# Attention and two dense blocks on one core: a list scheduler that treats VectorE and GpSimd as sharing one port exclusively, and float64 weights rebiased on ScalarE

## Chip, cores and metric

The kernel runs on one core of one Trainium2 chip. The metric is the device time of a launch in microseconds (us). Matmuls run on TensorE (PE in the rows), its weight loads beside them (PEld), elementwise work on VectorE (DVE), ScalarE (ACT) and GpSimd (POOL); transfers are issued from SyncE (SP).

## What is computed

Three stages, each fed by the one before; batch 4, widths as in the code:

```python
# 1: windowed attention with 32 global tokens (8 heads, 512 local tokens, head_dim 64)
s_g = scale * q_g @ concat(k_g, k_l).T;  out_g = softmax(s_g) @ concat(v_g, v_l)
s_ll = where(abs(i - j) <= 32, scale * q_l @ k_l.T, -1e9)
out_l = softmax(concat(scale * q_l @ k_g.T, s_ll)) @ concat(v_g, v_l)
x = concat(out_g, out_l) as (4, 576, 512)
# 2: first dense block, w_in (512, 1024), conv_w (3, 1024), w_out (1024, 512)
h = maximum(x @ w_in, 0)
gate = 1 / (1 + exp(-(3-tap convolution of h over the sequence)))
x = (h * gate) @ w_out
# 3: second dense block
xk = mu_k * x + (1 - mu_k) * x_prev;  xr = mu_r * x + (1 - mu_r) * x_prev
k = maximum(xk @ w_k, 0)
out = 1 / (1 + exp(-(xr @ w_r))) * ((k * k) @ w_v)
```

## The kernel before, in words

**Attention.** The 32 (batch, head) pairs are handled as 16 units of two heads, four units to a batch; unit u belongs to batch u // 4. For each unit `attend` issues scores (`s`, matmuls at L460 and L469), a masked minimum on VectorE (L484, eight passes of 128 columns), exponentials on ScalarE (L491), transposes of the exponentials (`pe`, L500), their copy to SBUF (`eT`, L503, ScalarE or VectorE), the product with v (`o`, L510), the division (L520 to L522, VectorE), a transpose (`X`, L541) and the split of x into a high and a low part (`xh`, L548, ScalarE or VectorE; `xl`, L551, VectorE). For each second unit `glob` does the same for the global tokens (`sg`, `eg`, `peg`, `egT`, `Xg`).

**First dense block,** `dense(b)` for each batch: eight H groups m (`ph`, matmuls at L856), relu (L880 on ScalarE, L882 on VectorE), a convolution of three taps (the first at L891, L893 or L895, on ScalarE, VectorE or GpSimd; the other two at L898 on VectorE), sigmoid (L904, ScalarE), a product `mu` (L907, VectorE or GpSimd) and the split of the gate into `gh` (L914, ScalarE or VectorE) and `gl` (L919, GpSimd or VectorE). Two m share one pair of gate tiles: `gh0_6` and `gl0_6` hold m = 6 and 7 of batch 0. Then the O matmuls (`po`, L957) need all gates; the results go to DRAM.

**Second dense block,** `moe2`: chunks of 384 tokens, the last of 256. Each has a K stage (`pk`, L1094, eight m, each followed by a relu at L1112 on ScalarE, a square at L1117 and a split into `k2h` and `k2l`, L1124 and L1129), an R stage (`pr`, L1160) and a V stage (`pv`, L1197) that needs `k2h` and `k2l`.

All dense matmuls are three products of high and low parts.

**Weights** come as float64, seen as pairs of 32-bit words. `narrow_tasks` (L701) makes fp32 of a piece of 128 x 512 (or 256) in passes: absolute value of the upper word (L712 on ScalarE, L714 on VectorE), max with a constant (L717, VectorE or GpSimd), a shift with a mask (L721, VectorE), and two passes that bring in the sign and the lower word's bits (L727, VectorE). A split into a high part (L792) and a low part (L795, GpSimd or VectorE) follows.

**Order.** All of this is recorded as tasks with an engine, a planned cost, alternatives on other engines, needs and buffers. `Plan.keys` gives due times, worked back from constants (`SLOT`, `LEAD`, `GAP`, `STEP0`, `LAG_TE`, `LAG_PV`, ...); `Plan.schedule` then takes, step by step, from the tasks that could start within `WINDOW` of the earliest start the one due first. For a task with alternatives it takes the engine with the earliest planned end plus a bias of the engine and phase (`DVE_BIAS`, `ACT_BIAS`, `POOL_BIAS`; five phases by `PHASES`). The tasks are emitted in that order under `manual_schedule`, so each engine runs its instructions in the planned order, and waits for what they need; planned times themselves enforce nothing. Before, a planned cost on VectorE or GpSimd grew by a factor (`PORT`, `POOL_SLOW`) for the time in which the other was planned busy (`shared`).

Of the kernel before, what the change touches and what calls it, by code (L numbers as in the profile page):

```python
# [54 lines left out]
H_FRAC = 0.5  # L55
LAG_TE = 5000
LAG_PV = 10538
LAG_G = 7061
# [1275 lines left out]
```

## Time and profile before

| | |
|---|---|
| median of 3 runs | 604.93 us (604.0 to 605.22) |
| profiled execution | 603.86 us |
| its span, first to last instruction | 602.1 us |
| mean granted TensorE clock | 0.949 |
| busy: PE, DVE, ACT, POOL | 565.3 us (94%), 395.7 (66%), 285.5 (47%), 228.2 (38%) |

Busy shares are of the span; PE's is no statement that TensorE works at full speed. A row of the chain of waits is a stretch in which the end of the program depended on that engine. Rows by line and form give busy time, mean duration and what ended the engine's idle time before them.

### The profile page before, as it was taken

What the parts mean: (1) busy time and instruction counts of PE and PEld (TensorE: products, weight loads), DVE (VectorE), ACT (ScalarE), POOL (GpSimd) and SP (SyncE); (2) the same over time, 40 slices, a digit from 0 to 9 for tenths busy, and PEclk for the clock granted to TensorE, in tenths of its full rate; (3) what the DMA queues carried; (4) which work ended last, traced back from release to release, by engine and by line L of the source; (5) the groups of instructions that cost most, each with busy time, mean ns of one, the idle gap of its engine ahead of it and who ended that gap; (6) DMA issues with size and microseconds to landing.
All of it is one profiled execution on the core that took longest, in us unless ns stands there. A gap on an engine that the chain in (4) does not pass through costs nothing. (4 is left out here: it accounts for less than half of the span.)

```text
span 602.1 us, 14503 instructions
## 1 busy us (share of the span) xinstructions
PE 565.3 (94%) x5790; PEld 515.3 (86%) x5790; DVE 395.7 (66%) x969; ACT 285.5 (47%) x632; POOL 228.2 (38%) x320
## 2 busy tenths in 40 slices
PE   8697957997999979999999899999999999999998
PEld 6585946996989879889899799889889899898897
DVE  3689999847699954999958976441826637434211
ACT  4585856614588623677466634504305225134040
POOL 3647767622243302333111554937602203203150
PEclk8787986797999979999999989999999999999999
DMA  8957701567515675005480432020110200100000
GB/s 310 339 195 246 275 10 52 179 180 233 179 54 197 193 255 174 20 3 167 170 255 16 137 126 64 8 81 18 39 67 1 62 35 1 53 19 1 36 19 35
DMA packets 34627, 67.80 MB, mean 113 GB/s; under 512 B 5120, under 2 KB 14592, under 8 KB 34560
## 3 DMA queue, kind: packets, MB, share of 16 engines
q1 hardware_dynamic: 34560, 66.88, 33.4%
q8 instruction: 45, 0.74, 0.5%
q14 instruction: 22, 0.18, 0.1%
HBM read 52.71 MB, written 14.16 MB: 111 GB/s over the span
## 5 line engine op out<-in xcount | busy, mean ns | idle before, releaser
L856 PE MATMUL ph<-x,win_hi 128*128 128x256 f32 (+1 forms) x512 | 102.4, 298 | 0.0
L957 PE MATMUL po<-gl,wout_hi 128*128 128x256 f32 (+1 forms) x256 | 77.8, 304 | 7.1 <-POOL gl L919 5.2
L957 PE MATMUL po<-gh,wout_hi 128*128 128x256 f32 (+1 forms) x256 | 79.9, 312 | 2.8 <-ACT gh L914 2.8
L856 PEld LDWEIGHTS ph<-x,win_hi 128*128 128x128 f32 x512 | 81.2, 192 | 1.4
L957 PE MATMUL po<-gh,wout_lo 128*128 128x256 f32 (+1 forms) x256 | 76.9, 300 | 0.0
L856 PE MATMUL ph<-x,win_lo 128*128 128x256 f32 (+1 forms) x256 | 74.2, 290 | 0.0
L1112 ACT ACTIVATE robuf<-pk 128x384 f32<-128x384 f32 (+1 forms) x48 | 22.7, 472 | 91.8 <-PE pk L1094 91.4
L898 DVE SCALAR_TENSOR_TENSOR c<-h,convw,c 128x544 f32<-128x544 f32 x64 | 60.2, 959 | 4.6 <-POOL h L877 2.3
L1094 PE MATMUL pk<-xkh,wkk_lo 128*128 128x384 f32 (+1 forms) x192 | 62.7, 327 | 0.0
L1094 PE MATMUL pk<-xkh,wkk_hi 128*128 128x384 f32 (+1 forms) x192 | 62.7, 327 | 0.0
L1094 PE MATMUL pk<-xkl,wkk_hi 128*128 128x384 f32 (+1 forms) x192 | 62.7, 327 | 0.0
L957 PEld LDWEIGHTS po<-gl,wout_hi 128*128 128x128 f32 x256 | 51.7, 202 | 8.0 <-POOL gl L919 5.9
L957 PEld LDWEIGHTS po<-gh,wout_hi 128*128 128x128 f32 x256 | 51.7, 202 | 4.5 <-ACT gh L914 3.2
L1197 PE MATMUL pv<-wvv_lo,k2h 128*128 128x512 f32 (+1 forms) x144 | 54.4, 378 | 0.0
L1197 PE MATMUL pv<-wvv_hi,k2h 128*128 128x512 f32 (+1 forms) x144 | 54.4, 378 | 0.0
L1197 PE MATMUL pv<-wvv_hi,k2l 128*128 128x512 f32 (+1 forms) x144 | 54.4, 377 | 0.0
L1210 DVE TENSOR_TENSOR robuf<-pv,robuf 128x512 f32<-128x512 f32 (+1 forms) x18 | 11.9, 661 | 63.5 <-PE pv L1197 63.4
L957 PEld LDWEIGHTS po<-gh,wout_lo 128*128 128x128 f32 x256 | 51.7, 202 | 0.0
L856 PEld LDWEIGHTS ph<-x,win_lo 128*128 128x128 f32 x256 | 49.0, 192 | 0.0
L491 ACT ACTIVATE e<-e 128x128 f32<-128x128 f32 x128 | 39.8, 392 | 8.8 <-DVE e L484 8.7
L1160 PE MATMUL pr<-wrr_hi,xrbuf 128*128 128x512 f32 x136 | 43.7, 395 | 0.0
L1094 PEld LDWEIGHTS pk<-xkl,wkk_hi 128*128 128x128 f32 x192 | 36.1, 188 | 0.2
(224 smaller groups left out, 1294.9 us busy)
## 6 DMA issues: line engine op xcount, KB each, us to landing
v<-in_v_l_dram SPq DMA_DIRECT2D x16, 910.0 KB, 7.1
x2d<-xo SPq DMA_DIRECT2D x16, 272.5 KB, 2.9
qT<-in_q_l_dram SPq DMA_DIRECT2D x16, 256.0 KB, 3.6
kT<-in_k_l_dram SPq DMA_DIRECT2D x16, 256.0 KB, 4.7
wout_0r<-in_moe_w_out_dram SPq DMA_DIRECT2D x8, 512.0 KB, 4.5
out_dram<-robuf SPq DMA_DIRECT2D x16, 256.0 KB, 2.0
win_0r<-in_moe_w_in_dram SPq DMA_DIRECT2D x4, 512.0 KB, 8.0
win_512r<-in_moe_w_in_dram SPq DMA_DIRECT2D x4, 512.0 KB, 7.3
```

The source lines that it names most:

```text
L491: nc.scalar.activation(be.tile[:, P * i : P * (i + 1)], be.tile[:, P * i : P * (i + 1)], AF.Exp, bias=be.tile[:, SL + i : SL + i + 1], sca ...
L856: nc.tensor.matmul(pm, lhsT=w[:, k, P * m : P * (m + 1)], rhs=x[:, s0:s1], start=(k == 0 and n == 0), stop=(k == KT - 1 and n == 2),)
L898: e.scalar_tensor_tensor(bc.tile, bh.tile[:, k : k + S], convw[:, FT * k + m : FT * k + m + 1], bc.tile, op0=ALU.mult, op1=ALU.add,)
L957: nc.tensor.matmul(pm, lhsT=w[:, k, P * m : P * (m + 1)], rhs=g[:, k % 2, s0:s1], start=(k == 0 and n == 0), stop=(k == FT - 1 and n == 2),)
L1094: nc.tensor.matmul(bp.tile[:, :n], lhsT=w[:, k, P * m : P * (m + 1)], rhs=x[:, :n], start=(k == 0 and i == 0), stop=(k == KT - 1 and i == 2),)
L1112: e.activation(kk()[:, :n], bp.tile[:, :n], AF.Relu)
L1160: nc.tensor.matmul(bp.tile, lhsT=x[:, P * j : P * (j + 1)], rhs=w[:, k], start=(k == 0 and i == 0), stop=(k == KT - 1 and i == 2),)
L1197: nc.tensor.matmul(bp.tile, lhsT=x, rhs=w[:, k, c0:c1], start=(k == 0 and i == 0), stop=(k == FT - 1 and i == 2),)
L1210: nc.vector.tensor_mul(o()[:, c0:c1], bp.tile, r()[:, c0:c1])
```

## The change

The planner gets a resource `PORT`: a planned pass of VectorE whose kind is in the set `PORT` holds it for its whole planned duration, one of GpSimd for 0.9 of it (0.5 for first taps and for the normalisation `gn`, 0 for a memset of ones), and neither starts, in the plan, before it is free. The factors go. In `narrow_tasks` the absolute value and the max are replaced by one ScalarE pass that multiplies the upper word, read as fp32, by 2^-112; the shift loses its mask, and the sign is taken with a mask of one bit. Constants of the due times and biases change. Lines up to 700 of before stand 5 lines higher after, those from 717 on 17 lines: L957 becomes L940, L919 L902, L898 L881, L795 L778, L727 L713 and L721 L709.

```diff
-F64_MIN = float(np.array(0x38000000, np.uint32).view(np.float32))
+REBIAS = 2.0**-112
...
-SLOT = 72484
-LEAD = 14181
+SLOT = 67927
+LEAD = 18186
...
-POOL_BIAS = (6, 0, 235, 0, 113)
+POOL_BIAS = (514, 564, 295, 354, -3480)
...
-                    if o[0] == "DVE":
-                        c = shared(c, free.get("POOL", 0.0) - x, PORT.get(t.kind, 1.0))
-                    elif o[0] == "POOL":
-                        c = shared(c, free.get("DVE", 0.0) - x if dve_port else 0.0, POOL_SLOW)
+                    if holds_port(o[0], t.kind):
+                        x = max(x, free.get("PORT", 0.0))
...
-            if t.eng == "DVE":
-                dve_port = PORT.get(t.kind, 1.0) > 1.0
+            if h := holds_port(t.eng, t.kind):
+                free["PORT"] = max(free.get("PORT", 0.0), t.start + h * t.cost)
...
-def shared(cost, left, slow):
-
-    if left <= 0:
-        return cost
-    return cost * slow if left >= cost * slow else left + cost - left / slow
+def holds_port(eng, kind):
+
+    if eng == "POOL":
+        return 0.0 if kind == "on" else 0.5 if kind in ("cv", "gn") else 0.9
+    return 1.0 if eng == "DVE" and kind in PORT else 0.0
...
-        def fabs(e):
+        def fmag():
             state["mag"] = alloc(bmag, [P, max(n, EST)], F32, f"{nm}m")[:, :n]
-            hw = state["raw"][:, :n, 1]
-            if e is nc.scalar:
-                e.activation(state["mag"], hw.bitcast(F32), AF.Abs)
-            else:
-                e.tensor_scalar(state["mag"].bitcast(I32), hw, 0x7FFFFFFF, None, op0=ALU.bitwise_and)
-
-        def fmax(e):
-            e.tensor_scalar(state["mag"], state["mag"], F64_MIN, None, op0=ALU.max)
+            nc.scalar.activation(state["mag"], state["raw"][:, :n, 1].bitcast(F32), AF.Copy, scale=REBIAS)
...
-            nc.vector.tensor_scalar(
-                bits, bits, 3, 0x3FFFFFF8, op0=ALU.logical_shift_left, op1=ALU.bitwise_and
-            )
+            nc.vector.tensor_scalar(bits, bits, 3, None, op0=ALU.logical_shift_left)
...
-        c = add("ACT", 40 + 480 * f, lambda: fabs(nc.scalar), deps=[a], take=[bmag], use=[braw], name=f"abs{nm}",
-                alts=[("DVE", 60 + 275 * f, lambda: fabs(nc.vector))])
-        c = add("DVE", 60 + 275 * f, lambda: fmax(nc.vector), deps=[c], use=[bmag], name=f"max{nm}",
-                alts=[("POOL", 70 + 1386 * f, lambda: fmax(nc.gpsimd))])
+        c = add("ACT", 90 + 490 * f, fmag, deps=[a], take=[bmag], use=[braw], name=f"abs{nm}")
         c = add("DVE", 60 + 275 * f, fshift, deps=[c], use=[bmag], name=f"shl{nm}")
-        c = add("DVE", 68 + 534 * f, lambda: for_(1, -0x40000000, ALU.bitwise_and), deps=[c],
+        c = add("DVE", 68 + 534 * f, lambda: for_(1, -0x80000000, ALU.bitwise_and), deps=[c],
```

The order of the instructions changes on every engine. Three places follow; names carry the unit or batch (`s8_0`: scores of unit 8, first half; `po0_0_0`: O of batch 0) and a buffer number.

TensorE behind the first O matmuls of batch 0, before; the first matmul that needs `gl0_6` follows only behind the scores of units 6 and 7:

```order
L957 MATMUL po0_1_1_1504<-gl0_0_1407,wout_hi_165 128x288
L957 MATMUL po0_1_1_1504<-gh0_0_1357,wout_lo_166 128x288
L510 MATMUL o4_1_1514<-v4_842,eT4_1_1002 32x65 x16
L500 MATMUL pe5_0_1533<-ident_94,e5_0_1075 128x128 x4
L500 MATMUL pe5_1_1540<-ident_94,e5_1_1091 128x128 x4
L638 MATMUL peg5_0_1554<-ident_94,eg5_1131 128x128 x3
L510 MATMUL o5_0_1561<-v5_1057,eT5_0_1549 32x65 x16
L510 MATMUL o5_1_1583<-v5_1057,eT5_1_1552 32x65 x16
L541 MATMUL X4_1605<-ident_94,xn4_1545 128x128 x4
L638 MATMUL peg5_1_1618<-ident_94,eg5_1131 128x128 x3
```

The changed kernel's TensorE, up to and into the first O matmuls of batch 0:

```order
L464 MATMUL s8_0_1722<-kT8_1180,qT8_1016 32x96 x4
L464 MATMUL s8_1_1723<-kT8_1180,qT8_1016 32x96 x4
L495 MATMUL pe6_1_1774<-ident_94,e6_1_1591 128x128 x4
L505 MATMUL o6_0_1781<-v6_1097,eT6_0_1765 32x65 x16
L495 MATMUL pe7_0_1809<-ident_94,e7_0_1676 128x128 x4
L505 MATMUL o6_1_1818<-v6_1097,eT6_1_1800 32x65 x16
L940 MATMUL po0_0_0_1837<-gh0_0_1321,wout_hi_165 128x256
L940 MATMUL po0_0_0_1837<-gl0_0_1560,wout_hi_165 128x256
L940 MATMUL po0_0_0_1837<-gh0_0_1321,wout_lo_166 128x256
```

Scores of unit 8 and the second stage of units 6 and 7 stand ahead of O where before units 4 and 5 did. Between here and the first matmul that needs `gl0_6` stand also the scores of unit 9 and the rest of units 6 to 8.

GpSimd while `w_out` is narrowed, before (`wout3_0m` is a piece of w_out in work, `c0_0` the conv and gate tile of m = 0):

```order
L717 TENSOR_SCALAR wout3_0m_1195<-wout3_0m_1195 128x512
L876 MEMSET h0_2_1217 128x1
L877 MEMSET h0_2_1217 128x1
L907 TENSOR_TENSOR c0_0_1170<-c0_0_1170,h0_0_1137 128x544
L895 TENSOR_SCALAR c0_1_1265<-h0_1_1181,convw_96 128x544
L717 TENSOR_SCALAR wout4_0m_1256<-wout4_0m_1256 128x512
L876 MEMSET h0_4_1287 128x1
L877 MEMSET h0_4_1287 128x1
L795 TENSOR_TENSOR wout_lo_166<-wout2_0m_1142,wout_hi_165 128x512
```

The same place after:

```order
L890 TENSOR_TENSOR c0_2_1237<-c0_2_1237,h0_2_1212 128x544
L859 MEMSET h0_6_1361 128x1
L860 MEMSET h0_6_1361 128x1
L859 MEMSET h0_5_1372 128x1
L860 MEMSET h0_5_1372 128x1
L778 TENSOR_TENSOR wout_lo_166<-wout0_0m_1078,wout_hi_165 128x512
L778 TENSOR_TENSOR wout_lo_166<-wout2_0m_1223,wout_hi_165 128x512
```

The max passes and first taps are gone there; products, low parts and memsets stay.

VectorE at the last conv taps of batch 0 (`c0_5` to `c0_7`), before, with the division of unit 5 (`xn5`) and the masks of unit 6 behind them:

```order
L898 SCALAR_TENSOR_TENSOR c0_5_1625<-h0_5_1409,convw_96,c0_5_1625 128x544
L898 SCALAR_TENSOR_TENSOR c0_7_1674<-h0_7_1446,convw_96,c0_7_1674 128x544
L898 SCALAR_TENSOR_TENSOR c0_5_1625<-h0_5_1409,convw_96,c0_5_1625 128x544
L898 SCALAR_TENSOR_TENSOR c0_7_1674<-h0_7_1446,convw_96,c0_7_1674 128x544
L520 TENSOR_SCALAR xn5_1614<-o5_1_1583 128x4
L521 RECIPROCAL xn5_1614<-xn5_1614 128x4
L522 TENSOR_TENSOR xn5_1614<-o5_1_1583,xn5_1614 128x4x64
L484 ISA e6_0_1717<-s6_0_1632,mask_95 128x128
L484 ISA e6_0_1717 128x1
```

The same place after:

```order
L881 SCALAR_TENSOR_TENSOR c0_5_1947<-h0_5_1372,convw_96,c0_5_1947 128x544
L881 SCALAR_TENSOR_TENSOR c0_6_1835<-h0_6_1361,convw_96,c0_6_1835 128x544
L881 SCALAR_TENSOR_TENSOR c0_7_1996<-h0_7_1435,convw_96,c0_7_1996 128x544
L881 SCALAR_TENSOR_TENSOR c0_5_1947<-h0_5_1372,convw_96,c0_5_1947 128x544
L881 SCALAR_TENSOR_TENSOR c0_7_1996<-h0_7_1435,convw_96,c0_7_1996 128x544
L479 ISA e9_0_2038<-s9_0_1949,mask_95 128x128
L479 ISA e9_0_2038 128x1
```

The taps are followed by the masks of unit 9 instead of unit 6.

## Rows read from the trace of the kernel before

**Rows 1.** Chain of waits, its end in order of time: start us, us, what.

```profile
346.75 17.19 PE po L957 x122
363.94 16.65 PE pk L1094 x96
380.59 8.39 PE pr L1160 x36
```

**Rows 2.** Windows: us, length, busy us of each engine, TensorE clock, DMA share, GB/s.

```profile
46.00:114.50 68.50, 55.07 (x648) 49.67 (x649) 66.42 (x127) 43.25 (x92) 52.16 (x56) 0.78 0.40 135
114.50:150.00 35.50, 31.83 (x419) 29.82 (x418) 21.85 (x80) 12.53 (x37) 9.79 (x18) 0.90 0.73 235
150.00:310.30 160.30, 154.64 (x2313) 143.57 (x2312) 130.56 (x417) 100.19 (x220) 47.22 (x91) 0.98 0.45 149
310.30:346.70 36.40, 33.49 (x263) 32.88 (x262) 31.95 (x42) 23.85 (x46) 11.57 (x27) 1.00 0.34 100
```

**Rows 3.** Timeline of GpSimd: start us, us, engine, line, operation, idle before.

```profile
87.61 1.52 POOL L919 TENSOR_TENSOR gl<-c,gh 128x544 fp32r<-128x544 f32 x1
...
113.18 1.34 POOL L919 TENSOR_TENSOR gl<-c,gh 128x544 fp32r<-128x544 f32 x1 [0.58 <-DVE gh L914]
```

**Rows 4.** Timeline of TensorE, two of its waits.

```profile
87.64 0.58 PE L957 MATMUL po<-gl,wout_hi 128*128 128x256 f32 x1 [4.02 <-POOL gl L919]
...
140.80 1.96 PE L510 MATMUL o<-v,eT 128*32 128x65 f32 x64 [3.67 <-ACT eT L503]
```

**Rows 5.** VectorE by line and form, 0 to 114.5 us: busy us, mean ns, idle.

```profile
L898 DVE SCALAR_TENSOR_TENSOR c<-h,convw,c 128x544 f32<-128x544 f32 x16 | 19.0, 1226 | 0.0
L727 DVE SCALAR_TENSOR_TENSOR wout_0m<-wout_0r,wout_0m 128x512 int32<-128x512 int32 x16 | 17.4, 1098 | 0.0
L484 DVE CUSTOM_DVE_ANT_0 e<-s,mask 128x128 f32<-128x128 f32 x56 | 12.6, 284 | 9.7 <-PE s L469 9.7
L727 DVE SCALAR_TENSOR_TENSOR win_0m<-win_0r,win_0m 128x512 int32<-128x512 int32 x8 | 8.2, 1048 | 0.1
L727 DVE SCALAR_TENSOR_TENSOR win_512m<-win_512r,win_512m 128x512 int32<-128x512 int32 x8 | 7.0, 899 | 0.0
...
L717 DVE TENSOR_SCALAR wout_0m<-wout_0m 128x512 f32<-128x512 f32 x4 | 4.0, 1008 | 0.0
L551 DVE TENSOR_TENSOR x<-X,x 128x512 fp32r<-128x512 f32 x5 | 3.4, 679 | 0.0
```

**Rows 6.** Timeline of VectorE, single passes.

```profile
65.48 0.78 DVE L898 SCALAR_TENSOR_TENSOR c<-h,convw,c 128x544 f32<-128x544 f32 x1
...
67.84 0.68 DVE L727 SCALAR_TENSOR_TENSOR wout_0m<-wout_0r,wout_0m 128x512 int32<-128x512 int32 x1
...
82.43 0.41 DVE L717 TENSOR_SCALAR wout_0m<-wout_0m 128x512 f32<-128x512 f32 x1
...
87.85 1.82 DVE L727 SCALAR_TENSOR_TENSOR wout_0m<-wout_0r,wout_0m 128x512 int32<-128x512 int32 x1
```

**Rows 7.** ScalarE by line and form, 0 to 114.5 us.

```profile
L712 ACT ACTIVATE wout_0m<-wout_0r 128x512 f32<-128x512 f32 x8 | 5.4, 675 | 1.3 <-DMA wout_0r<-in_moe_w_out_dram 1.3
```

**Rows 8.** Timeline of TensorE, pieces of attention at full clock.

```profile
235.00 1.08 PE L460 MATMUL s<-gT,qT 64*128 64x32 f32 x16
236.01 1.00 PE L469 MATMUL s<-kT,qT 64*32 64x96 f32 x64
...
240.06 0.60 PE L500 MATMUL pe<-ident,e 128*128 128x128 f32 x4
...
243.26 0.66 PE L510 MATMUL o<-v,eT 128*32 128x65 f32 x32
...
269.76 1.59 PE L653 MATMUL Xg<-egT,v 96*64 96x32 f32 x48
```

**Rows 9.** GpSimd by line and form, 388 to 599 us.

```profile
L1129 POOL TENSOR_TENSOR k2l<-robuf,k2h 128x384 fp32r<-128x384 f32 x13 | 14.7, 1147 | 2.9 <-ACT k2h L1124 2.9
L1117 POOL TENSOR_TENSOR robuf<-robuf 128x384 f32<-128x384 f32 x10 | 8.7, 874 | 11.4 <-ACT robuf L1112 11.4
```

More of the change, by code (lines that the diff above doesn't have):

```diff
@@ L46 @@
 T_START = 10000
-STEP0 = 6737
+STEP0 = 7625
 T_DENSE = 38000
-SLOT = 72484
-LEAD = 14181
-GAP = 2397
+SLOT = 67927
+LEAD = 18186
+GAP = -7615
 GAP1 = 1480
@@ L54 @@
 E_BUFS = 4
[L55 to L58, printed above, removed]
+H_FRAC = 0.498
+LAG_TE = 3810
+LAG_PV = 10413
+LAG_G = 5305
 LEAD_Q = 4000
@@ L64 @@
 LAG_TX = 9367
-WINDOW = 43
+WINDOW = 46
 FILL_MIN = 553
@@ L69 @@
 FILL_RATE = 0.478
-PENALTY = 166
+PENALTY = -75
 PHASES = (60e3, 105e3, 320e3, 375e3)
-DVE_BIAS = (1550, 807, 684, 1523, 580)
-ACT_BIAS = (411, 657, 466, 1004, 80)
-POOL_BIAS = (6, 0, 235, 0, 113)
+DVE_BIAS = (1550, 1239, 579, 1523, 550)
+ACT_BIAS = (411, 685, -139, 215, 80)
+POOL_BIAS = (514, 564, 295, 354, -3480)
 H_BUFS = 5
@@ L212, in schedule @@
         free["PE"] = 1130.0
-        dve_port = False
         while cand:
@@ L304 @@
 WEIGHTS = ("win", "wout", "wkk", "wrr", "wvv", "conv")
-POOL_SLOW = 1.17
 PORT = {
-    "cv": 1.55, "mu": 1.65, "gl": 1.65, "gh": 3.0, "max": 1.6, "shl": 1.6, "sgn": 1.15, "low": 1.15, "lo": 1.65,
-    "hi": 3.0, "d": 1.65, "xxk": 1.9, "xxr": 1.9, "xkh": 3.0, "xrh": 3.0, "xkl": 1.65, "xrl": 1.65, "sq": 1.65,
-    "k2h": 3.0, "k2l": 1.65, "gn": 2.0,
-}
-def shared(cost, left, slow):
-    if left <= 0:
-        return cost
-    return cost * slow if left >= cost * slow else left + cost - left / slow
+    "cv", "mu", "gl", "gh", "max", "shl", "sgn", "low", "lo", "hi", "d", "xxk", "xxr", "xkh", "xrh", "xkl", "xrl", "sq",
+    "k2h", "k2l", "gn",
+}
+def holds_port(eng, kind):
+    if eng == "POOL":
+        return 0.0 if kind == "on" else 0.5 if kind in ("cv", "gn") else 0.9
+    return 1.0 if eng == "DVE" and kind in PORT else 0.0
 def bias(eng, x):
```

## Prediction, made before the change was run

> **What bounds the kernel now.** I read the chain of waits first. From 346.75 us on it holds nothing but TensorE: O matmuls of batch 3 until 363.94, then the K, R and V stages of the six chunks without a break [rows 1]. That tail, 235 us to the last store, cannot get shorter by work taken off other engines; only its start can move. What the change can earn lies before 347 us.
>
> Next the windows by stage [rows 2]. From 46 to 114.5 us VectorE is busy for 66.42 of 68.5 us. TensorE is busy for 55.07 and its granted clock is 0.78, so it does the work of 55.07 × 0.78 = 43 us at full clock and has 25 us to spare. From 114.5 to 150 us the clock is 0.90 and TensorE idles 3.67 us, from 150 to 310.3 us 5.7 us at 0.98, from 310.3 to 346.7 us 2.9 us at 1.00. So one stretch is bound by VectorE, and the rest almost by TensorE. The first stretch ends where batch 0's last gate does: GpSimd's pass at 113.18 takes 1.34 and ends at 114.52 [rows 3]; O of batch 0 needs it.
>
> TensorE's waits tell what feeds it: 4.02 us for GpSimd's `gl` at 87.64, 3.67 us for ScalarE's copy of `eT` at 140.80 [rows 4].
>
> Last, VectorE's passes in that stretch. The same instruction has two durations: the conv tap L898 takes 0.78 at 65.48 and 1.226 in the mean, L727 takes 0.68 at 67.84 and 1.82 at 87.85 [rows 5, 6]. The 1.82 begin 0.24 after a GpSimd pass of 1.52 (87.61) and end 0.54 after it [rows 3, 6]: GpSimd holds VectorE up. The sum of that loss, mean against alone: 19.0 − 16 × 0.78 = 6.5 (L898), 17.4 − 16 × 0.68 = 6.5, 8.2 − 8 × 0.68 = 2.8 and 7.0 − 8 × 0.68 = 1.6 (L727), 4.0 − 4 × 0.41 = 2.4 (L717): 19.8 us [rows 5, 6]. Up to 114.5 us GpSimd runs 47 passes of 256 columns or more, so 0.42 us each.
>
> **The change, part by part.** The sum is made against the profiled execution, 603.86 us; the median of the runs shown, 604.93, is 1.07 above, and the forecast adds that at the end. A measurement can tell about 0.2%, 1.2 us, from no change.
>
> *Narrowing.* Abs and max become one ScalarE pass. In the whole program VectorE loses 22 max and 13 abs, GpSimd 35 max; ScalarE goes from 44 passes to 57. How long ScalarE's multiplication takes no row shows; the nearest is abs by the same engine over the same 512 columns, 0.675 [rows 7], and the conv's first tap, also a scaled copy, stands on ScalarE in the program already. I take 0.675 and charge the 13 passes with ScalarE below. Dropping the mask from the shift leaves its pass in place: nothing.
>
> *The order up to batch 0's last gate.* The list scheduler now forbids VectorE's port passes and GpSimd's to overlap, and by that and new constants fills VectorE otherwise. Ahead of that gate VectorE gets 24 more mask passes (0.284 each, 6.8), 15 more passes of 512 columns (4 copies of `eT`, 2 `xh`, 3 `xl`, 1 `lo`, and 5 divisions, each taken with its two small passes as one: at the 0.679 of `xl` 10.2) and 2 more gate products, priced as the conv tap (0.78, 1.6). It loses 4 max (0.41 alone), 2 abs, a shift, a relu and a `gh`, all taken at that price: 9 × 0.41 = 3.7. Net 6.8 + 10.2 + 1.6 − 3.7 = +14.9 us of VectorE [rows 5, 6]. GpSimd runs 30 passes there where it ran 47: 12 of the 13 max that go are the weights', and it keeps 14 `lo`, 6 `gl`, 6 products, 2 first taps and 2 `gn`. If each costs VectorE 0.42 as before, 17 × 0.42 = 7.2 comes back. The gate ends 14.9 − 7.2 = **7.7 us** later. The ends: GpSimd's passes cost VectorE nothing any more (30 × 0.42 = 12.6 less), or the loss stays at 19.8 (7.2 more). I keep the price per pass because the row of the one pair and the total both come from this stretch.
>
> What TensorE gets for it: ahead of the first matmul that needs that gate now also stand the scores of units 8 and 9, the transposes and products of units 6, 7 and 8, X of 6 and 7 and one Xg. At full clock scores take 1.08 + 1.00, a half's transpose or an X 0.60, a half's product 0.66, Xg 1.59 [rows 8]: 2 × 2.08 + 8 × 0.60 + 6 × 0.66 + 1.59 = **14.5 us** of later work done early. The room for it is the 25 us that TensorE has to spare in the stretch, which itself gets 7.7 longer. So the gate comes 7.7 later and 14.5 us less remain behind it.
>
> *114.5 to 150 us.* TensorE loses 3.67 idle and 0.10 × 31.83 = 3.2 by the clock [rows 2]. With two units of attention ahead, O of batch 0 has its gates and H of batch 1 its inputs without the wait for `eT`. I take 6 of 6.9. Cover gone: if ScalarE falls behind, `eT` waits as before and the term is 0.
>
> *150 to 310.3 us.* 5.7 idle and 0.02 × 154.6 = 3.1 by the clock [rows 2]. GpSimd's gates (`gl`) of batches 1 and 2 go from 6 and 4 to 1 and 3, its first conv taps from 6 and 7 to none, which ScalarE (100.19 busy of 160.3) and VectorE (130.56) take. VectorE's share rises; I take 3 of 8.8, with 0 and 6 as ends.
>
> *End of batch 3.* 2.9 idle [rows 2]. The last gates there ran on GpSimd and VectorE; now GpSimd has no large pass in batch 3. I take 2, with 0 as the end.
>
> *The tail.* GpSimd takes nearly all of the squares and of their low parts: 44 of 48 each, from 20 and 27. One m of stage K then costs it 0.874 + 1.147 = 2.02 us [rows 9] against 16.65 / 8 = 2.08 of TensorE [rows 1]. It keeps up, barely; what it falls behind the 8.39 us of stage R behind each K covers [rows 1]. If the two passes stretch to 2.5 us, GpSimd is 8 × 0.4 = 3.4 late, still under 8.39: nothing. DMAs are the same but for one.
>
> **Sum:** +14.9 − 7.2 − 14.5 − 6 − 3 − 2 = −17.8, so 586.1 for the profiled execution and 587.1, say **587 us**, for the median.
>
> **A rule against the trace.** The pair of rows says that a VectorE pass that begins during a GpSimd pass loses 1.14 of the latter's 1.52; all 47 passes together, some 70 us by 1.5 each, cost 19.8 [rows 3, 5, 6]. The Trainium skill ("SBUF — State Buffer", section "Who interferes with whom") says that the two engines share one port pair, taken for a whole instruction, and that whoever comes second fully blocks; a VectorE instruction with two inputs in SBUF contends with GpSimd's reads. By that rule the pair agrees, the total only where VectorE had other passes to run.
>
> **Rivals.**
> 1. *ScalarE becomes the bound (slower).* Ahead of the gate ScalarE gets 33 more instructions (160 to 193): 16 exponentials, 3 table loads and 14 others. In the stretch 92 took 43.25 us, 0.47 each, so +15.5: 58.8 us of work [rows 2]. ScalarE sits between VectorE's passes in every chain (mask, exponential, copy; conv, sigmoid, product) and reached 43.25 / 68.5 = 63% there. At that share 58.8 us take 93 us, the gates come 24.6 later, and 14.5 + 6 + 3 + 2 = 25.5 are just paid back: 63% is the point from which it decides. At 57%, with the queue blocked at its head by longer chains, 103 us: 34.6 − 25.5 = +9, 614 us. For it: between the last conv pass and the gate VectorE now also has unit 9's masks. Against it: VectorE, not ScalarE, was full before.
> 2. *The port costs nothing any more.* Orders that keep port passes apart take the other 12.6 away: 574 us. For it: the planner now treats it as exclusive. Against it: its planned times are not the chip's, nothing but the order is enforced.
> 3. *It doesn't do what it says.* Fewer passes, each held up longer: the loss stays 19.8, 7.2 more: 594 us. For it: the `gl` and `lo` passes that stay read two operands each and are the long ones, 1.52 against VectorE's 0.68.
> 4. *Each remaining pass blocks VectorE for its whole length:* 30 × 1.5 = 45 in place of 12.6, +32: 619 us. The total of before, 19.8 instead of 70, speaks against it [rows 5]. It is the rule of the Trainium skill's section named above, taken for every pass.
>
> **How the numbers follow.** Forecast 0.54 (by the ends of the terms behind the gate 582, with 6.9, 6 and 2.9, to 593, where `eT` waits as before); rival 1 0.13; rival 2 0.12; rival 3 0.13; rival 4 0.03; gains and losses that cancel to within 1.2 us 0.05. Faster: 0.54 + 0.12 + 0.13 = 0.79; same 0.05; slower 0.13 + 0.03 = 0.16. The range goes from 570, rival 2 with the stretches behind the gate at their lower ends, to 605, which takes in rival 3 and no change; rivals 1 and 4 stay out, with a few hundredths below 570.
>
> **What would show it.** In the profile after: batch 0's last gate ends near 122 us; the chain reaches pure TensorE at about 329 us in place of 346.75, with a tail of the same length behind; VectorE's L713 and L881 means in the first stretch fall toward 0.68 and 0.78 but not to them; no wait of over 3 us between that gate and 150 us; ScalarE's rebiasing passes take 0.6 to 0.75. A last gate at 138 us or later with ScalarE over 60% busy would be rival 1; a mean of L881 that stays at 1.2, rival 3; TensorE waiting for `k2l` in stage V would break the tail's term.

## The result, and the profile after

The changed kernel takes 580.47 us in the median of four runs (572.21 to 581.89), before 605.08 beside it: a ratio of 0.9547 (95% interval 0.9446 to 0.9647). Six more runs of the same file give 582.3 us (575.5 to 584.6) and 0.9616 (0.9569 to 0.9664). Executions of this one order differ by up to 12 us, and with them the mean granted clock (0.965 to 0.988), so two versions of it are told apart only from some 3 us on. The profiled execution took 580.47 us with a span of 578.3 and a mean clock of 0.970.

The chain of waits of the changed kernel, its end in order of time, with the two pieces ahead of it:

```profile
275.31 1.52 PE Xg L648 x48
276.83 0.59 PE X L536 x4
277.42 14.45 PE po L940 x114
291.87 24.11 PE ph L839 x192
315.97 24.12 PE po L940 x192
340.09 16.65 PE pk L1077 x96
356.74 8.39 PE pr L1143 x36
```

The first K stage begins at 340.09 us in place of 363.94 [rows 1], 23.85 earlier; from there to the end it is 238.2 us in both (578.3 − 340.09 and 602.1 − 363.94). All of the gain lies ahead of the second dense block, and from 277 us on the chain is nothing but TensorE: H and O of batch 3 run without a stop.

Windows of the changed kernel, cut at the end of batch 0's last gate (columns as in [rows 2]):

```profile
0.00:46.00 46.00, 39.23 (x876) 33.79 (x884) 28.59 (x139) 28.65 (x76) 11.30 (x32) 0.89 0.82 299
46.00:121.50 75.50, 68.99 (x1165) 60.93 (x1144) 67.16 (x193) 60.13 (x134) 32.58 (x48) 0.89 0.48 163
121.50:150.00 28.50, 28.50 (x229) 28.50 (x230) 14.11 (x46) 10.87 (x32) 0.86 (x9) 1.00 0.72 233
150.00:277.00 127.00, 121.97 (x1837) 112.21 (x1837) 104.48 (x325) 92.02 (x198) 11.67 (x48) 0.97 0.42 137
277.00:340.00 63.00, 63.00 (x503) 63.00 (x502) 48.99 (x86) 39.71 (x80) 1.65 (x23) 1.00 0.51 157
```

Two windows of before that the rows ahead of the prediction left out, and a part of the second:

```profile
0.00:46.00 46.00, 37.99 (x823) 31.59 (x823) 28.85 (x131) 27.63 (x75) 22.63 (x38) 0.85 0.77 278
310.30:363.90 53.60, 50.64 (x386) 50.03 (x386) 42.73 (x53) 29.03 (x59) 18.99 (x35) 0.97 0.35 105
347.00:364.00 17.00, 17.00 (x124) 17.00 (x124) 10.57 (x12) 5.28 (x13) 7.12 (x9) 0.90 0.34 111
```

What TensorE loses in each stretch, its idle time plus what the clock takes of its busy time (busy × (1 − clock)), shows where the gain came from:

| stretch (before / after) | before | after | difference |
|---|---|---|---|
| 0 to 46 | 8.0 + 5.7 = 13.7 | 6.8 + 4.3 = 11.1 | −2.6 |
| 46 to the last gate of batch 0 | 13.4 + 12.1 = 25.5 | 6.5 + 7.6 = 14.1 | −11.4 |
| from there to 150 | 3.7 + 3.2 = 6.9 | 0 | −6.9 |
| 150 to 310.3 / 277 | 5.7 + 3.1 = 8.8 | 5.0 + 3.7 = 8.7 | −0.1 |
| to the first K, 363.9 / 340 | 3.0 + 1.5 = 4.5 | 0 | −4.5 |

The sum is −25.5 against 23.85 on the chain; the clock is printed to two places, which over 300 us explains such a rest.

The gate itself comes later. Timelines of GpSimd and VectorE in the changed kernel, the passes that end `gl` of batch 0:

```profile
117.61 1.34 POOL L902 TENSOR_TENSOR gl<-c,gh 128x544 fp32r<-128x544 f32 x1 [1.34 <-ACT gh L897]
```

```profile
117.98 1.56 DVE L902 TENSOR_TENSOR gl<-c,gh 128x544 fp32r<-128x544 f32 x1
120.80 0.72 DVE L902 TENSOR_TENSOR gl<-c,gh 128x544 fp32r<-128x544 f32 x1
```

It ends at 121.52 where it ended at 114.52 [rows 3]. From 46 us to the gate VectorE is busy 0.7 us longer than before (67.16 against 66.42) and idles 6.3 us more (8.3 against 2.1): the later gate is nearly all idle time of VectorE. The first of VectorE's two passes, 0.72 alone, took 1.56: it ran into the GpSimd pass above, which ended at 118.95.

VectorE by line and form up to that gate:

```profile
L881 DVE SCALAR_TENSOR_TENSOR c<-h,convw,c 128x544 f32<-128x544 f32 x16 | 14.6, 939 | 1.3 <-ACT c L874 1.2
L713 DVE SCALAR_TENSOR_TENSOR wout_0m<-wout_0r,wout_0m 128x512 int32<-128x512 int32 x16 | 11.6, 752 | 0.0
...
L713 DVE SCALAR_TENSOR_TENSOR win_0m<-win_0r,win_0m 128x512 int32<-128x512 int32 x8 | 5.3, 685 | 0.0
...
L713 DVE SCALAR_TENSOR_TENSOR win_512m<-win_512r,win_512m 128x512 int32<-128x512 int32 x8 | 5.2, 684 | 0.0
```

Against 0.78 and 0.68 alone these lose 14.6 − 12.5 = 2.1, 11.6 − 10.9 = 0.7 and nothing: under 3 us where the same four groups lost 6.5 + 6.5 + 2.8 + 1.6 = 17.4 [rows 5, 6].

Those four groups are not all that meets GpSimd. The shifts (L709), the low parts that VectorE makes (L778), its products (L890) and its gate parts (L902) in the changed kernel, up to the gate:

```profile
L709 DVE TENSOR_SCALAR wout_0m<-wout_0m 128x512 int32<-128x512 int32 x8 | 5.2, 665 | 0.4 <-ACT wout_0m L705 0.2
...
L709 DVE TENSOR_SCALAR win_512m<-win_512m 128x512 int32<-128x512 int32 x4 | 2.7, 688 | 0.0
L778 DVE TENSOR_TENSOR wout_lo<-wout_0m,wout_hi 128x512 fp32r<-128x512 f32 x2 | 2.6, 1312 | 0.0
...
L709 DVE TENSOR_SCALAR win_0m<-win_0m 128x512 int32<-128x512 int32 x4 | 2.5, 632 | 0.4 <-ACT win_0m L705 0.4
L890 DVE TENSOR_TENSOR c<-c,h 128x544 f32<-128x544 f32 x2 | 2.3, 1145 | 0.0
L902 DVE TENSOR_TENSOR gl<-c,gh 128x544 fp32r<-128x544 f32 x2 | 2.3, 1138 | 0.0
```

The same before, shifts at L721:

```profile
L721 DVE TENSOR_SCALAR wout_0m<-wout_0m 128x512 int32<-128x512 int32 x8 | 4.3, 563 | 0.0
...
L721 DVE TENSOR_SCALAR win_0m<-win_0m 128x512 int32<-128x512 int32 x4 | 3.1, 768 | 0.9 <-POOL win_0m L717 0.9
...
L721 DVE TENSOR_SCALAR win_512m<-win_512m 128x512 int32<-128x512 int32 x4 | 1.7, 416 | 0.0
L919 DVE TENSOR_TENSOR gl<-c,gh 128x544 fp32r<-128x544 f32 x2 | 1.6, 822 | 0.0
```

Alone these passes take 0.41 (shift, max), 0.72 (product, `gl`) and 0.68 (low part). The 16 shifts lose 3.8 us after and 2.5 before; the low parts, products and `gl` lose 3.0 after and 0.2 before; the max, gone after, lost 2.4. Over all these wide passes the loss falls from 22.4 to 9.3 us: by 13 us, more than half, and part of the collisions has only moved to other passes.

ScalarE's rebiasing, from 0 to 121.5 us, costs what the absolute value cost [rows 7]:

```profile
L705 ACT ACTIVATE wout_0m<-wout_0r 128x512 f32<-128x512 f32 x8 | 5.5, 684 | 0.7 <-DMA wout_0r<-in_moe_w_out_dram 0.7
```

### The profile page after: what moved, and what is told of

Read it like the earlier page. It is cut to its first block, busy times and chain, and to the rows that moved or that the text cites. A ratio compares the mean times of both kernels' runs of the same rounds, so it can differ in the third digit from the quotient of the medians.

```text
span 578.3 us, 14518 instructions
## 1 busy us (share of the span) xinstructions
PE 557.0 (96%) x5792; PEld 509.1 (88%) x5792; DVE 329.3 (57%) x889; ACT 303.7 (53%) x673; POOL 186.1 (32%) x304
## 4 chain that ended last, share of the span: by engine, by line
PE 52%; DVE 2%; ACT 0%; issue 0%; ACTq 0%
PE pk L1077 16%; PE pv L1180 16%; PE pr L1143 8%; PE po L940 7%; PE ph L839 4%; DVE c L881 1%; DVE e L479 0%; PE Xg L648 0%; PE o L505 0%; DVE ewvv_256m L709 0%; PE peg L633 0%; DVE ewvv_256m L713 0%; ACT eg L621 0%; DVE eg L599 0%; DVE c L890 0%
## 5 line engine op out<-in xcount | busy, mean ns | idle before, releaser
L940 PE MATMUL po<-gh,wout_hi 128*128 128x288 f32 (+1 forms) x256 | 76.5, 299 | 2.9 <-DVE eT L498 2.2
L940 PE MATMUL po<-gl,wout_hi 128*128 128x288 f32 (+1 forms) x256 | 74.1, 290 | 0.0
L839 PE MATMUL ph<-x,win_lo 128*128 128x288 f32 (+1 forms) x256 | 73.9, 289 | 0.0
L940 PE MATMUL po<-gh,wout_lo 128*128 128x288 f32 (+1 forms) x256 | 73.7, 288 | 0.0
L1100 POOL TENSOR_TENSOR robuf<-robuf 128x384 f32<-128x384 f32 (+1 forms) x44 | 35.6, 812 | 73.9 <-ACT robuf L1095 73.9
L881 DVE SCALAR_TENSOR_TENSOR c<-h,convw,c 128x544 f32<-128x544 f32 x64 | 52.6, 833 | 5.7 <-ACT c L874 5.1
L940 PEld LDWEIGHTS po<-gh,wout_hi 128*128 128x128 f32 x256 | 48.6, 190 | 4.4 <-DVE eT L498 2.4
L940 PEld LDWEIGHTS po<-gh,wout_lo 128*128 128x128 f32 x256 | 48.6, 190 | 0.0
L940 PEld LDWEIGHTS po<-gl,wout_hi 128*128 128x128 f32 x256 | 48.6, 190 | 0.0
L1112 POOL TENSOR_TENSOR k2l<-robuf,k2h 128x384 fp32r<-128x384 f32 (+1 forms) x44 | 42.6, 984 | 7.3 <-ACT k2h L1107 7.3
```

Of the source, the lines that this page charges most:

```text
L839: nc.tensor.matmul(pm, lhsT=w[:, k, P * m : P * (m + 1)], rhs=x[:, s0:s1], start=(k == 0 and n == 0), stop=(k == KT - 1 and n == 2),)
L881: e.scalar_tensor_tensor(bc.tile, bh.tile[:, k : k + S], convw[:, FT * k + m : FT * k + m + 1], bc.tile, op0=ALU.mult, op1=ALU.add,)
L940: nc.tensor.matmul(pm, lhsT=w[:, k, P * m : P * (m + 1)], rhs=g[:, k % 2, s0:s1], start=(k == 0 and n == 0), stop=(k == FT - 1 and n == 2),)
L1100: e.tensor_mul(ks()[:, :n], kk()[:, :n], kk()[:, :n])
L1112: e.tensor_sub(bg[1].tile[:, m % 2, :n], ks()[:, :n], bg[0].tile[:, m % 2, :n].bitcast(F32))
```

## The experiments

Each stands beside runs of before on its own chip. The ratio to those is the number to compare; us are medians.

| run | us | ratio (95%) | last gate | loss of the four groups | loss of all wide passes | GpSimd passes |
|---|---|---|---|---|---|---|
| before | 603.6 to 606.4 | 1 | 114.5 | 17.4 | 22.4 | 47 |
| `after_again` | 582.3 | 0.962 (0.957 to 0.966) | 122.8 | | 8.5 | 30 |
| `b_newnarrow` | 598.1 | 0.990 (0.987 to 0.993) | 113.7 | 16.2 | 18.7 | 34 |
| `a_oldconst` | 587.5 | 0.972 (0.967 to 0.977) | 116.4 | 3.7 | 6.9 | 39 |
| `a_shared` | 593.5 | 0.983 (0.977 to 0.990) | 111.6 | 12.1 | 16.9 | 31 |
| `a_oldnarrow` | 594.1 | 0.985 (0.981 to 0.988) | 131.5 | | 12.2 | 30 |
| `a_tail` | 585.1 | 0.969 (0.965 to 0.974) | 127.9 | | 10.1 | 30 |
| `a_lo2` | 588.5 | 0.975 (0.971 to 0.979) | 128.7 | 8.3 | 16.7 | 44 |
| `a_lo1` | 588.0 | 0.974 (0.970 to 0.979) | 129.8 | 5.6 | 12.2 | 44 |
| `a_act2` | 590.7 | 0.977 (0.972 to 0.981) | 125.6 | | 5.6 | 30 |
| `a_warmA` | 586.3 | 0.968 (0.963 to 0.972) | 125.0 | | 9.9 | 30 |
| `a_warmB` | 606.2 | 1.002 (0.998 to 1.005) | 142.4 | | 7.3 | 30 |
| `a_cvpool` | 584.7 | 0.966 (0.963 to 0.969) | 126.2 | | 10.2 | 36 |

The loss is that of the conv taps and of the passes that bring in sign and low bits of `w_out` and `w_in`, up to the last gate: busy time less 16 × 0.78 and 32 × 0.68. All wide passes are these and the shifts, max, low parts, products and `gl` of 512 or 544 columns. Gate and losses are those of one profiled execution each. Those of `a_oldnarrow`, `a_tail`, `a_cvpool` and `a_lo1` began with TensorE's granted clock at 0.51 to 0.73 from 24 to 43 us, the others of the changed kernel's order at 0.91 or 1.00, so gates are compared only between executions that began alike.

### The changed kernel again

> The changed kernel once more, unchanged, in five rounds. Three of its four times lie at 580 to 582 us and one at 572, with a mean granted clock of 0.988 against 0.970 to 0.979. If the spread is TensorE's clock alone, further runs fall into the same two groups, the low ones with a clock near 0.988 and all with a tail of 238 us behind the first K matmul. If the 572 was something else, say an early start of a transfer, no second one appears or its clock is not higher.

Four of its six times lie at 581.5 to 584.6, with clocks of 0.965 to 0.974, and two at 575.5 and 576.7, with 0.982 and 0.979; the profiled one, at 583.1, has a clock of 0.965. The first K begins at 342.8 us there and the tail is again 238.2. So the spread goes with the clock, and in this profile it lies ahead of the tail. No second run came near 572, and that run has no trace. One place where it arises is seen with `a_tail` below.

### The new narrowing alone, in before's order

```diff
-                e.activation(state["mag"], hw.bitcast(F32), AF.Abs)
+                e.activation(state["mag"], hw.bitcast(F32), AF.Copy, scale=REBIAS)
...
-            e.tensor_scalar(state["mag"], state["mag"], F64_MIN, None, op0=ALU.max)
+            pass
...
-                bits, bits, 3, 0x3FFFFFF8, op0=ALU.logical_shift_left, op1=ALU.bitwise_and
+                bits, bits, 3, None, op0=ALU.logical_shift_left
...
```

> Before's order on every engine, with the new narrowing put into it: rebiasing in the place of the absolute value, no max at all, a shift without a mask. Theory 'less work': the gain of the change is mostly the passes that go; 4 max of 1.0 us leave VectorE ahead of the last gate and 13 GpSimd passes at 0.42 us of loss each, 9.5 us, so the gate ends at about 105 us in place of 114.5 and the time falls by 7 to 10 us, to 595 to 598. Theory 'order': without the new order the stalls behind the gate stay and TensorE's queue still holds O of batch 0 in front of the attention, so less than half of the 24 us comes, 0 to 10. Rival 'only the order counts': under 3 us.

About 6 us faster (0.990). But the gate moves by 0.8 us only, to 113.7, not by 9: 13 GpSimd passes are gone and VectorE's loss is not. VectorE by line and form up to that gate, in before's order with the new narrowing:

```profile
L727 DVE SCALAR_TENSOR_TENSOR wout_0m<-wout_0r,wout_0m 128x512 int32<-128x512 int32 x16 | 19.2, 1211 | 0.1
L898 DVE SCALAR_TENSOR_TENSOR c<-h,convw,c 128x544 f32<-128x544 f32 x16 | 16.9, 1094 | 1.0 <-ACT c L891 1.0
```

L727's mean even rises from 1.098 to 1.211 [rows 5]. The four groups lose 16.2 us in place of 17.4, with 34 passes in place of 47; over all wide passes it is 18.7 in place of 22.4, and 2.4 of that fall are VectorE's own max passes, which went. A price per GpSimd pass, on which the forecast's first term rested, does not describe this.

### The old arithmetic in the changed order

```diff
-            nc.scalar.activation(state["mag"], state["raw"][:, :n, 1].bitcast(F32), AF.Copy, scale=REBIAS)
+            nc.scalar.activation(state["mag"], state["raw"][:, :n, 1].bitcast(F32), AF.Abs)
...
+            nc.vector.tensor_scalar(state["mag"], state["mag"], F64_MIN, None, op0=ALU.max)
-            nc.vector.tensor_scalar(bits, bits, 3, None, op0=ALU.logical_shift_left)
+            nc.vector.tensor_scalar(bits, bits, 3, 0x3FFFFFF8, op0=ALU.logical_shift_left, op1=ALU.bitwise_and)
...
```

> The changed kernel's order on every engine, with the old arithmetic in it: ScalarE takes the absolute value, VectorE a max just ahead of each shift, 57 passes more on VectorE, 17 of them ahead of batch 0's last gate. At 0.41 us alone that is 7 us there. Theory 'less work' expects the gate at 128 us in place of 121.5 and the time up by 6 to 10 us, to 587 to 590. If VectorE is no longer the bound of that stretch (8.4 of 76 us idle between 46 and 122 us), it is under 4 us.

Some 12 us slower than the changed kernel (0.985 against 0.962), more than expected. Its profiled execution began like that of `a_tail`, with TensorE at half clock from 24 to 43 us, so these two are compared: the gate at 131.5 against 127.9, 3.6 later, and the first K 9 us later (356.6 against 347.4). Some 4 of the other 5.6 us fall between 229 and 273 us, where VectorE narrows `w_v` and TensorE waits 2.0 us for its division, 0.3 in `a_tail`; windows of that stage, here and in `a_tail`:

```profile
229.00:273.00 44.00, 41.99 (x607) 38.73 (x606) 38.09 (x118) 32.63 (x65) 3.40 (x20) 0.92 0.29 94
```

```profile
225.00:265.00 40.00, 39.65 (x608) 36.30 (x607) 36.36 (x111) 31.93 (x64) 3.41 (x20) 1.00 0.33 105
```

So the old arithmetic costs more in an order that counts on its absence (9 us by these two profiles, 12 by the medians) than its removal brings in an order that was made with it (6). The two are not the same passes, though: here VectorE does all 57 max, where before GpSimd did 35 of them.

### The tail's old split between VectorE and GpSimd

```diff
-POOL_BIAS = (514, 564, 295, 354, -3480)
+POOL_BIAS = (514, 564, 295, 354, 113)
```

> The changed kernel with the last GpSimd bias put back from -3480 to 113, which moves squares and low parts of the last chunks from GpSimd back to VectorE and touches nothing ahead of the second dense block. The prediction priced the tail's move at nothing: within 1 us of the changed kernel, and a tail of 238.2 us from the first K matmul to the end in both. Rival: GpSimd falls behind TensorE there, and the tail is longer in the changed kernel.

The tail is 238.2 us long (585.6 − 347.4), as in the changed kernel and in before: that GpSimd takes 44 of 48 squares and low parts costs and brings nothing. Those passes in the changed kernel, by line, from 340 to 578 us:

```profile
L1112 POOL TENSOR_TENSOR k2l<-robuf,k2h 128x384 fp32r<-128x384 f32 (+1 forms) x44 | 42.6, 984 | 7.3 <-ACT k2h L1107 7.3
L1100 POOL TENSOR_TENSOR robuf<-robuf 128x384 f32<-128x384 f32 (+1 forms) x44 | 35.6, 812 | 73.9 <-ACT robuf L1095 73.9
```

The 3 us by which this kernel is slower arose ahead of any instruction that the edit touches; the intervals of the two ratios overlap. The same order began otherwise. From 24 to 43 us, in `a_tail` and in the changed kernel:

```profile
24.00:43.00 19.00, 19.00 (x255) 16.28 (x254) 13.12 (x70) 10.38 (x30) 2.64 (x5) 0.51 0.67 216
```

```profile
24.00:43.00 19.00, 17.02 (x400) 14.81 (x401) 15.66 (x78) 14.71 (x41) 5.16 (x7) 0.91 0.81 281
```

TensorE is busy throughout at half clock in the one, at 0.91 in the other, and the one's gate ends 6.4 us later. Up to 413 us both run the same instructions in the same order, so this is a spread between executions of one order. It is not the only place: `after_again` is at 1.00 from 24 to 43 us and loses its clock from 46 us to its gate (0.83 against the changed kernel's 0.89).

### The planner's rule and the constants, apart

The changed kernel planned by before's factors:

```diff
-                    if holds_port(o[0], t.kind):
-                        x = max(x, free.get("PORT", 0.0))
+                    if o[0] == "DVE":
+                        c = shared(c, free.get("POOL", 0.0) - x, PORT.get(t.kind, 1.0))
+                    elif o[0] == "POOL":
+                        c = shared(c, free.get("DVE", 0.0) - x if dve_port else 0.0, POOL_SLOW)
...
```

> The changed kernel with its constants and its narrowing, but planned by the factors of before in the place of the exclusive port; the order differs from the second unit on. In before's order with 13 GpSimd passes fewer VectorE still lost some 16 us to GpSimd ahead of the last gate, in the changed order, with nearly as many passes, under 5 in the same groups. Theory 'port kept apart': with the factors the loss is back above 12 us in those groups, and the time lies 5 to 15 us above the changed kernel's 582, at 587 to 597. Rival 'constants': the retuned due times and biases make the order, the planner's port rule little: within 4 us of 582.

The changed kernel with before's constants:

```diff
-SLOT = 67927
-LEAD = 18186
-GAP = -7615
+SLOT = 72484
+LEAD = 14181
+GAP = 2397
...
```

> The changed kernel's planner and narrowing with every constant of before (due times, window, penalty, biases). Theory 'port kept apart': the loss of VectorE to GpSimd ahead of the last gate stays low, under 6 us in the conv taps and narrowing passes, and the time falls clearly below before's order with the new narrowing (598): 583 to 592. Rival 'constants': it stays at 595 to 603, since the attention is due as late as before and batch 0's gates go first.

The theory of the port kept apart holds in both. VectorE by line and form up to the last gate, planned by the factors, and by the exclusive port with old constants:

```profile
L886 DVE SCALAR_TENSOR_TENSOR c<-h,convw,c 128x544 f32<-128x544 f32 x16 | 18.7, 1188 | 0.0
L718 DVE SCALAR_TENSOR_TENSOR wout_0m<-wout_0r,wout_0m 128x512 int32<-128x512 int32 x16 | 15.0, 972 | 0.0
```

```profile
L881 DVE SCALAR_TENSOR_TENSOR c<-h,convw,c 128x544 f32<-128x544 f32 x16 | 14.3, 924 | 0.0
L713 DVE SCALAR_TENSOR_TENSOR wout_0m<-wout_0r,wout_0m 128x512 int32<-128x512 int32 x16 | 11.9, 779 | 0.0
```

12.1 us of loss in the four groups with 31 GpSimd passes under the factors, 3.7 with 39 under the exclusive rule; over all wide passes 16.9 and 6.9: what decides is when the passes run, not how many. Yet the kernel planned by the factors has the earliest gate of all, 111.6, and is some 11 us slower than the changed one (593.5 against 582.3). Windows from 46 us to the last gate, under the factors and under the exclusive rule with old constants, tell why:

```profile
46.00:111.60 65.60, 50.93 (x588) 46.97 (x587) 63.59 (x127) 46.38 (x92) 36.32 (x45) 0.79 0.38 127
```

```profile
46.00:116.40 70.40, 62.53 (x1050) 56.62 (x1050) 61.68 (x185) 54.39 (x116) 43.14 (x55) 0.90 0.51 171
```

Under the factors TensorE does 50.93 × 0.79 = 40 us of full-clock work ahead of the gate, under the exclusive rule 62.53 × 0.90 = 56, in the changed kernel 68.99 × 0.89 = 61: attention is moved ahead. Up to its gate the kernel planned by the factors has run 560 score matmuls and 384 products with v, as many as before; the changed kernel has run 800 and 576. The rule alone, with the changed constants, is worth some 11 us (593.5 to 582.3), the constants some 5 (587.5 to 582.3). From before's order with the new narrowing to the rule with the same old constants it is also some 11 (598.1 to 587.5), but that step holds a second change: the one order was planned with the max passes in it, the other without. The factors with the old constants, planned without the max passes, were not run.

### What a GpSimd pass costs that the order isn't planned for

```diff
+                    if e is nc.gpsimd and nm in ("win", "wout"):
+                        nc.gpsimd.tensor_sub(w["lo"][:, k, c : c + WST], state["mag"], w["hi"][:, k, c : c + WST].bitcast(F32))
                     e.tensor_sub(w["lo"][:, k, c : c + WST], state["mag"], w["hi"][:, k, c : c + WST].bitcast(F32))
```

> The changed kernel's order, with each low part of w_in and w_out that GpSimd makes computed twice by it: 14 passes more of two SBUF operands, 128x512, ahead of batch 0's last gate, and each low part one pass later. GpSimd has room (32.6 of 76 us busy from 46 to 122). By the forecast's price of 0.42 us per pass VectorE loses 6 us more, and the gate ends some 6 later; if two-operand passes are the ones that hold VectorE up, by up to their whole length, it loses 10 to 20; if the order keeps them apart anyhow, under 3.

```diff
+                        nc.gpsimd.tensor_scalar(w["lo"][:, k, c : c + WST], state["mag"], 0.0, None, op0=ALU.max)
```

> As the kernel with the low parts made twice, but the pass ahead of each is a max with zero, of one SBUF operand and the same size, as the max passes were that the change took from GpSimd; the low part that follows is the right one. Taking 13 of them from before's order gave VectorE nothing back (its loss in the conv taps and L727 stayed at 16 us). If passes of one operand cost VectorE less than those of two, its loss here is clearly below that of the other kernel, by 4 us or more; if a pass is a pass, the two agree within 2 us.

The loss of the four groups rises from 2.5 to 8.3 us with 14 passes of two operands, 0.41 each, and to 5.6 with passes of one, 0.22 each; over all wide passes from 9.3 to 16.7 and 12.2, 0.53 and 0.21 each. The gate of `a_lo2`, which began like the changed kernel, ends 7.2 us later. The time is the same (588.5 and 588.0, +6), so the kinds can't be told apart by it, and not all of the time of `a_lo1` can be put on the port: each low part also comes one pass later in both. That each pass blocks VectorE for its whole 1.5 us, the last rival, is refuted; that they cost nothing in this order, too.

### ScalarE doubled

```diff
-            nc.scalar.activation(state["mag"], state["raw"][:, :n, 1].bitcast(F32), AF.Copy, scale=REBIAS)
+            for _ in range(2):
+                nc.scalar.activation(state["mag"], state["raw"][:, :n, 1].bitcast(F32), AF.Copy, scale=REBIAS)
```

> The changed kernel's order with each rebiasing pass issued twice on ScalarE: 16 passes of 0.68 us more ahead of batch 0's last gate, 11 us, in a stretch (46 to 122 us) in which ScalarE is busy for 60.6 of 76 us, and 41 more by the end. If ScalarE bounds that stretch (the prediction's slower rival, with its share as a ceiling), the gate ends 9 to 14 us later and the time is 590 to 596. If it sits in the chains but has slack, the gate moves by 2 to 5 us and the time by less than 6, to 583 to 588.

The gate ends 4.1 us later than in the changed kernel's profile (125.6), 2.8 later than in `after_again`, as the theory of slack had it; the time is up by 8 to 10, as the other had it. The rest arises behind the gate: up to the first K TensorE idles 10.2 us where it idled 5.0 in the changed kernel and 6.3 in `after_again`; its longest wait, for a copy of `eT`, is 3.7 us in place of 1.9 and 2.3. ScalarE doesn't bound the stretch ahead of the gate, but more work on it costs time behind.

### Fillers for the clock

```diff
-            warm(s[0][:, 0])
+            warm(s[0][:, 0], plan.fill + (36 if u == 2 else 0))
```

> The changed kernel with 36 filler matmuls ahead of the scores of unit 2, where TensorE waits 2.1 us for a transfer at 13.7 us; after that wait its granted clock is at half for 5 to 8 us. Runs of the same order differ by 10 us, and their mean clock with them (0.959 to 0.988). If the wait sets the clock there, the clock holds at 1.0 up to 24 us, the gate comes 2 to 4 us earlier and the time falls by as much, to 577 to 580. If the half clock comes from the light matmuls that follow, or just moves on, no difference beyond the spread of 3 us.

```diff
-            warm(s[0][:, 0])
+            warm(s[0][:, 0], plan.fill + (36 if u == 2 else 8 if 3 <= u <= 9 else 0))
...
-                warm(o.rearrange("p i d -> p (i d)"))
+                warm(o.rearrange("p i d -> p (i d)"), plan.fill + (8 if 2 <= u <= 8 else 0))
```

> As the kernel with 36 fillers ahead of unit 2's scores, and 8 fillers more ahead of the scores of units 3 to 9 and of each product with v of units 2 to 8: 168 more, 9 us of TensorE at full clock in a stretch in which it has room. The clock from 24 to 60 us, 0.57 to 0.99 in the runs so far, should stay above 0.9 in every run. If TensorE's clock in the first 60 us is what spreads the runs, the time is 572 to 577 with little spread; if that stretch hangs on VectorE and ScalarE, the fillers cost what they take, and the time is 582 or more.

The clock does what was hoped. In `a_warmA` it is 1.00 from 16 to 22 us, where the changed kernel, behind its wait of 2.1 us, has 0.51; in `a_warmB` it is 1.00 from 46 to 122 us and 0.994 over the span. The time does not follow: 586.3 and 606.2 us. Window and fillers of `a_warmB`, up to 130 us:

```profile
46.00:122.00 76.00, 74.66 (x1184) 69.43 (x1183) 53.89 (x149) 50.97 (x114) 25.77 (x42) 1.00 0.44 156
```

```profile
L353 PE MATMUL s<-ident 128*128 128x128 f32 x190 | 23.7, 282 | 0.0
L353 PE MATMUL o<-ident 128*128 128x128 f32 x176 | 21.8, 277 | 0.4 <-ACT eT L498 0.4
```

An fp32 filler is two records, 0.25 us, not the 0.05 that the expectation had counted. 45 us of fillers in a stretch in which TensorE is busy for 69 of 75.5 us put the gate 21 us later (142.4). In the changed kernel TensorE has little room there, too. The 36 fillers of `a_warmA` are 9 us by that price in a wait of 2.1, and its gate ends 3.5 later than the changed kernel's.

### First taps from ScalarE to GpSimd

```diff
-alts=[("ACT", 640, lambda fc0=fc0: fc0(nc.scalar))
+alts=[("ACT", 640, lambda fc0=fc0: fc0(nc.gpsimd))
```

> The changed kernel's order with the 26 first conv taps that ScalarE does (0.75 us each) done by GpSimd in their place, 6 of them ahead of batch 0's last gate, 19.5 us off ScalarE in all; GpSimd has room and its own first tap took 0.72 alone. Issuing 16 passes of 0.68 more on ScalarE ahead of that gate cost some 9 us of time. If ScalarE is what the changed kernel hangs on there and behind, this is faster by 2 to 6 us, 576 to 580. If the price of GpSimd's passes beside VectorE, 0.2 to 0.4 us each where the order isn't planned for them, takes it back, within 2 us of 582; if first taps now wait in GpSimd's queue behind its long passes, slower, 584 to 590.

Not told apart from the changed kernel (0.966 against 0.962, overlapping). Beside `a_tail`, which began at a like clock, the first K is at 347.4 us in both. VectorE's conv taps take 1.023 in the mean where they took 0.939, up to the gate: some of what ScalarE gains is paid at the port. No version beat the changed kernel.

## Why the prediction was right, and where it was not

Forecast 587 us (570 to 605), measured 580.5 and 582.3: right in sign and range, some 5 us too high. It took 1.2 us for what a measurement can tell; executions of the changed order differ by up to 12. Step by step:

- *The gate 7.7 us later.* It ended 7.0 later, but that the two agree is luck. Of the 7.0 us VectorE's work made 0.7 and its idle time 6.3; it was busy for 66.42 of 68.5 us before [rows 2] and now idles 8.3 of 75.5, with 3.5 in one wait for TensorE's `pe`. The step "each costs VectorE 0.42 as before" failed: the loss fell by 13 us over all wide passes (15 in the four groups), not by 7.2; before's order with 13 passes fewer lost 16.2 in the four groups, the exclusive rule left 3.7 with 39. The sum of 19.8 had also left out the shifts, which lost 2.5 more. Rival 2, that the port costs nothing any more, was nearer for the four groups (2.5 left) than for all wide passes (9.3 left), and its gain did not come as an earlier gate, since VectorE was no longer full.
- *14.5 us of attention done early.* Mis-sized, and the largest miss. Up to the gate TensorE did 37.99 × 0.85 + 55.07 × 0.78 = 75.3 us of full-clock work before and 39.23 × 0.89 + 68.99 × 0.89 = 96.3 after: 21 more. The list left out scores of a third unit (800 score matmuls ran up to the gate where 560 did), 24 of the global units' `sg` and 6 of their `peg`: it was counted by instructions ahead of a matmul, not by what was done when the gate ended. Net of the gate's delay 14 us were gained, not 6.8. That it is the early attention that pays, not an early gate, `a_shared` bears out.
- *114.5 to 150 us, 6.* Right: 6.9, no idle time left.
- *150 to 310.3 us, 3.* Wrong: 8.8 before, 8.7 after. The waits there are TensorE's for `e` and `eT` (2.1 and 1.9 us in the changed kernel), chains that fewer GpSimd passes did not shorten; in `a_act2` the longest wait for `eT` is 3.7.
- *End of batch 3, 2.* Mis-sized: 4.5. The prediction took all from 346.75 us on for fixed. But O of batch 3 took 17.19 us for 122 matmuls [rows 1], at a clock of 0.90, behind its wait; at 24.12 / 192 each it would take 15.3. A stretch that is all TensorE is not yet one at full clock. The chain is pure TensorE from 277 us on, not from about 329. The three terms behind the gate, 11 us forecast, came to 11.5 together; that their errors cancel is luck.
- *The tail, nothing; rebiasing at 0.675 each.* Right: 238.2 us, 0.684.
- *Rival 1,* ScalarE as the bound with 63% as its share: it reached 60.13 / 75.5 = 80%, so the ceiling was no ceiling. *Rival 3,* that the loss stays, is what happens without the exclusive rule (`b_newnarrow`, 16.2; `a_shared`, 12.1). *Rival 4:* above.

By parts: the narrowing 6 us in before's order, the exclusive rule some 11, the constants some 5. These are differences of versions planned anew, so the parts depend on the order in which they are taken; taken out last, the narrowing is worth 9 to 12.

## What to carry to other kernels

Where two engines hold each other up, count the overlaps that the order makes, not the passes: with 13 GpSimd passes gone VectorE still lost 18.7 of 22.4 us, planned apart it lost 6.9 to 9.3. Sum such a loss over all passes that can collide: in the four groups that were watched it fell by more than four fifths, since part of it had moved to others. Judge a reordering by the bottleneck engine's work that is done when a gate opens, not by when it opens: the version with the earliest gate took some 11 us longer than the changed kernel. And ahead of calling a stretch fixed, compare its time per matmul with one at full clock.
